# Attention with plain float32 products on quarter and half tiles of the TensorE array, and an instruction order from a list scheduler

## Chip, cores and metric

The kernel runs on one core of a Trainium2 chip. The metric is device time in microseconds (us) of one execution of the whole program; lower is better. Engines are called as in the profile: PE is TensorE's matrix multiply, PEld its weight load, DVE VectorE, ACT ScalarE, POOL GpSimd, SP the queue that issues the transfers.

## What is computed

Sixteen head pairs (4 batches, 8 heads, 576 tokens, 64 features per head) go through attention with a threshold, and the 2304 tokens by 512 features that come out go through two feed-forward layers with 2048 hidden columns. All in float32; weights arrive as float64.

```python
def _attn_ref(q, k, v, tau):
    scale = 1.0 / np.sqrt(q.shape[-1])
    scores = scale * np.matmul(q, k.transpose(0, 1, 3, 2))
    thresh = np.max(scores, axis=-1, keepdims=True) - tau
    scores = np.where(scores >= thresh, scores, -1000000000.0)
    scores = scores - np.max(scores, axis=-1, keepdims=True)
    attn = np.exp(scores)
    attn = attn / (np.sum(attn, axis=-1, keepdims=True) + 1e-09)
    return np.matmul(attn, v).astype(np.float32)

def _moe_ref(x, w_in, w_out):        # first layer
    h = x @ w_in
    g = h * np.cos(h)
    return (g @ w_out).astype(np.float32)

def _moe2_ref(x, w_in, w_out, s, b): # second layer
    h = x @ w_in
    r = np.maximum(h, 0.0)
    g = s * (r * r) + b
    return (g @ w_out).astype(np.float32)
```

## The kernel before

**Attention** (lines 207 to 569). A head pair is one unit of work. Its 1152 queries lie in nine tiles of 128 (tile 4 holds the last 64 queries of both heads). For each tile PE forms the scores against 576 keys in two halves of 288 (`scores`, L368, tile `s`); DVE takes the minimum over the row (`stat`, L380; the scores have their sign turned), a threshold is made from it (`limit`, L389 on DVE or L387 on ACT), ACT takes the exponential (`expo`, L394), and DVE masks it and sums the row in one instruction (`mask`, L406, tile `p`). PE turns `p` through an identity (`transposes`, L460 and L468), ACT copies it out of PSUM (`copies`), and PE multiplies it by the values (`weighted`, L519 for the first head, L528 for the second). The sums go through a reciprocal, a PE transpose and a trip through DRAM (`spread`) to multiply the result (`normalise`, L552 on POOL).

Most products run as float32r passes: an operand x is split into x_hi (rounded) and x_lo = x - x_hi, and the passes are added. For the scores the query's two parts lie on the two halves of the 128 rows (`qs`), the keys lie twice, and two passes per half of the keys do (`kh`, `kl`). For the second head the turned probabilities and the values are split as well (`ph`, `pl`, `vs`). The splits are made on POOL, ACT and DVE (`prep`; `lows`, L509; `pool_high`, `pool_low`). For the first head alone, L519 is a plain float32 product, which fills 64 of the array's 128 columns.

**Layers** (lines 597 to 757). Tokens go in blocks of 512 (one of 256). A step is one block of 128 hidden columns: 12 products into a hidden bank (`hidden`, L662), a chain on DVE, ACT and POOL (`activate`), and 12 products into the accumulators two steps later (`output`, L716 in the first layer, L718 in the second). A layer needs 32 weight halves. Each is loaded as float64 (`wr`), decoded by one ACT and four DVE instructions (`decode`, L157, L159, L161, L165, L169), rounded on ACT (`wh`, L191) and reduced to its low part on POOL (`wl`, L135). Thirteen halves are decoded during attention, 19 of the first layer after it, beside the first block; the second layer's 32 are decoded beside the last block of the first layer and the first block of the second.

**Order.** Every instruction carries a due time from a table of tuned numbers (`ORDER`, `AFTER`, `DEC`, `PACE`), and a heap emits them by that time. Each engine executes its own list strictly in that order. The scores have three PSUM tiles of two banks each, shared with the weighted values; the turned probabilities have two banks.

## Time and profile before

| what | value |
|---|---|
| median of 3 runs | 1205.75 us (1203.57 to 1205.77) |
| span of the profiled execution | 1204.2 us |
| attention, first to last row minimum or mask on DVE | 8.7 to 355 us, 21.6 us per head pair |
| first block of the first layer, to its last output product | 494.7 us |
| from there to the end | 709.5 us |
| busy over the span | PE 94%, DVE 68%, ACT 47%, POOL 46% |

The page gives shares over the whole span, which mixes stages: in attention DVE is busy nearly all of the time and PE nine tenths of it; in the layers PE is busy all of the time, except beside the two stretches in which weights are decoded. So the stages are read apart below. Busy times of PE overlap, since a record's end is modelled: what one product costs is read from the distance between starts.

### The profile page before, as it was taken

To read this page: it belongs to the slowest core of one execution; us is meant where nothing else is said; L and a number is where in the kernel's file an instruction comes from. 1 tells how busy PE (TensorE), PEld (TensorE's weight loads), DVE (VectorE), ACT (ScalarE), POOL (GpSimd) and SP (SyncE) were. 2 spreads that over 40 slices of the span, in tenths; PEclk is the share of its full clock that TensorE was granted. 3 is DMA by queue.
4 is the path that set the end of the run, shared out by engine and by line. 5 is a ranking of instruction groups with operands and counts; after the bars stand their busy time and mean duration, and the time that the engine had idled before them with its cause. 6 is when DMAs were issued, how large, how long until landed. Compare 5 with 4: busy or idle time off the path is not lost.

```text
span 1204.2 us, 16262 instructions
## 1 busy us (share of the span) xinstructions
PE 1129.5 (94%) x5808; PEld 918.3 (76%) x5808; DVE 821.5 (68%) x1410; ACT 568.8 (47%) x1069; POOL 555.3 (46%) x531
## 2 busy tenths in 40 slices
PE   6998888989998888999999999999999999999998
PEld 5676667677675666788998887778888889888886
DVE  7799999999987999645665479998861133212211
ACT  6787777878874444223332244454442233222222
POOL 6687887887865544222222235444542222222221
PEclk9899999999999899999999999999999999999999
DMA  5233333342212232000000012322220000000000
GB/s 155 80 111 110 97 100 121 97 129 92 80 37 80 88 106 90 16 1 1 1 2 1 1 34 94 101 84 91 88 71 1 1 36 1 18 1 1 36 1 35
DMA packets 30416, 68.76 MB, mean 57 GB/s; under 512 B 5232, under 2 KB 9728, under 8 KB 30336
## 3 DMA queue, kind: packets, MB, share of 16 engines
q1 hardware_dynamic: 30192, 67.72, 17.8%
q8 instruction: 46, 0.75, 0.3%
q14 instruction: 34, 0.28, 0.1%
q10 hardware_dynamic: 144, 0.00, 0.0%
HBM read 62.92 MB, written 4.79 MB: 56 GB/s over the span
## 4 chain that ended last, share of the span: by engine, by line
PE 60%; DVE 31%; issue 5%; ACT 2%; DMA 1%; POOL 1%; SPq 0%; DVEq 0%; ACTq 0%; POOLq 0%
PE acc L718 16%; PE hs L662 14%; PE ht L662 13%; PE acc L716 10%; DVE p L406 6%; DVE r L231 5%; DVE mn L380 5%; PE s L368 3%; PE pt L468 3%; DVE wt L161 2%; DVE thr L389 2%; DVE wt L159 2%; DVE wt L169 2%; DVE wt L165 2%; DVE r L679 2%
## 5 line engine op out<-in xcount | busy, mean ns | idle before, releaser
L135 POOL TENSOR_TENSOR gl<-r,gh 128x512 fp32r<-128x512 f32 (+1 forms) x160 | 194.6, 1217 | 435.9 <-DVE gh L231 222.3
L662 PE MATMUL hs<-x,wh 128*128 128x512 f32 (+1 forms) x640 | 187.0, 375 | 20.1 <-DVE r L231 16.2
L679 DVE TENSOR_SCALAR r<-r,s_t,b_t 128x512 f32<-128x512 f32 (+1 forms) x80 | 42.5, 531 | 180.4 <-ACT r L682 180.4
L662 PE MATMUL ht<-x,wh 128*128 128x512 f32 (+1 forms) x560 | 158.6, 368 | 0.0
L662 PEld LDWEIGHTS hs<-x,wh 128*128 128x128 f32 x640 | 117.5, 191 | 47.1 <-DVE r L231 19.0
L368 PE MATMUL s<-kh,qs 128*128 128x288 f32 x320 | 105.7, 346 | 38.1 <-DVE p L406 32.9
L135 POOL TENSOR_TENSOR wl<-wt,wh 128x512 fp32r<-128x512 f32 x60 | 81.4, 1358 | 111.8 <-ACT wh L191 104.8
L662 PE MATMUL hs<-x,wl 128*128 128x512 f32 (+1 forms) x320 | 119.1, 372 | 0.0
L394 ACT ACTIVATE e<-s,mn 128x576 f32<-128x576 f32 x144 | 105.8, 735 | 28.1 <-DVE mn L380 26.7
L716 PE MATMUL acc<-gl,wh 128*128 128x512 f32 (+1 forms) x300 | 111.8, 373 | 6.6 <-POOL gl L135 6.6
L406 DVE SCALAR_TENSOR_TENSOR p<-s,thr,e 128x576 f32<-128x576 f32 x144 | 115.2, 807 | 1.3 <-ACT e L394 0.9
L662 PEld LDWEIGHTS ht<-x,wh 128*128 128x128 f32 x560 | 102.0, 188 | 18.1
L380 DVE TENSOR_REDUCE mn<-s 128x1 f32<-128x576 f32 x144 | 108.2, 752 | 7.8 <-PE s L368 6.3
L682 ACT ACTIVATE r<-r,hpi 128x512 f32<-128x512 f32 (+1 forms) x80 | 54.3, 679 | 122.2 <-DVE r L231 122.2
L716 PE MATMUL acc<-gh,wh 128*128 128x512 f32 (+1 forms) x300 | 111.0, 370 | 0.3 <-ACT gh L682 0.2
L716 PE MATMUL acc<-gh,wl 128*128 128x512 f32 (+1 forms) x300 | 110.6, 369 | 0.0
L368 PEld LDWEIGHTS s<-kh,qs 128*128 128x128 f32 x320 | 63.5, 198 | 59.5 <-issue 26.2
L718 PE MATMUL acc<-wh,gh 128*128 128x512 f32 x270 | 105.2, 390 | 0.0
L718 PE MATMUL acc<-wh,gl 128*128 128x512 f32 x270 | 105.2, 390 | 0.0
L718 PE MATMUL acc<-wl,gh 128*128 128x512 f32 x270 | 105.0, 389 | 0.0
L662 PE MATMUL ht<-x,wl 128*128 128x512 f32 (+1 forms) x280 | 103.0, 368 | 0.0
L468 PE MATMUL pt<-ident,p 128*128 128x128 f32 (+1 forms) x640 | 93.4, 281 | 1.9 <-ACT ph L487 1.2
(97 smaller groups left out, 2399.5 us busy)
## 6 DMA issues: line engine op xcount, KB each, us to landing
wr<-in_w_dram SPq DMA_DIRECT2D x64, 512.0 KB
k<-in_kt_dram SPq DMA_DIRECT2D x32, 288.0 KB
q<-in_qt_dram SPq DMA_DIRECT2D x15, 320.0 KB
q<-in_qt_dram SPq DMA_DIRECT2D x16, 288.0 KB
out_dram<-ob SPq DMA_DIRECT2D x18, 256.0 KB
v<-in_va_dram SPq DMA_DIRECT2D x16, 160.0 KB
v<-in_vb_dram SPq DMA_DIRECT2D x16, 160.0 KB
rb<-rd SPq DMA_DIRECT2D x16, 144.0 KB
```

The costliest lines, as they stand in the source:

```text
L135: (eng or nc.gpsimd).tensor_tensor(out=o, in0=a, in1=b.bitcast(F32), op=ALU.subtract)
L231: heapq.heappush(todo, (key, next(count), lambda: fn(*args)))
L368: nc.tensor.matmul(st[:, h, :H2], qs[:, c : c + 128], kx[:, o + h * H2 : o + (h + 1) * H2], start=(j == 0), stop=(j == len(ops) - 1),)
L380: nc.vector.tensor_reduce(out=mn, in_=sv, axis=mybir.AxisListType.XY, op=ALU.min)
L394: nc.scalar.activation(e, sv, AF.Exp, bias=mn, scale=-1.0)
L406: nc.vector.scalar_tensor_tensor(out=p, in0=sv, scalar=thr, in1=e, op0=ALU.is_le, op1=ALU.mult, accum_out=sm[:, i : i + 1])
L468: nc.tensor.transpose(pt[:kw, j * 128 : (j + 1) * 128], src[:, k * 128 : k * 128 + kw], ident)
L662: nc.tensor.matmul(h, w[:, c * P : (c + 1) * P], x, start=(c == 0 and j == 0), stop=(c == HP - 1 and j == 2))
L679: nc.vector.tensor_scalar(out=o, in0=x, scalar1=a, scalar2=b, op0=ALU.mult, op1=ALU.add)
L682: nc.scalar.activation(o, x, fn, **kw)
L716: nc.tensor.matmul(acc[d][:, :n], w[:, d * P : (d + 1) * P], g, **st)
L718: nc.tensor.matmul(acc[d], g[:, d * P : (d + 1) * P], w, **st)
```

## The change

- All of attention's products become plain float32. No operand of attention is split, so `prep`, `lows`, `pool_high`, `pool_low`, `vc` and `gather` go.
- **Tiles of the array.** The keys' two halves now lie on the two halves of the rows: one product per half contracts 64 rows (tile of 64 rows by 128 columns). Turning is done in pieces of 64 queries, each half of the queries on its half of the rows; the last 64 keys of all tiles are turned by products on quarter tiles (64 by 64, `turn_rest`). The weighted values of the two heads use the two halves of the columns (128 by 64).
- **Places.** The threshold (`limit`), the sums' small addition, the keys' scaling, the weights' clamp and the clamp of the first layer's activation go to POOL. ACT copies all turned probabilities out of PSUM.
- **Buffers.** The scores have two PSUM tiles in place of three, the weighted values one of their own. Eight weight halves have places from the start and are decoded during attention in place of thirteen; the other 24 follow.
- **Order.** A list scheduler (`Order`) places every instruction with a length, a rank, dependences and ring tickets, and emits by planned start.

```diff
+class Order:
...
+    def add(self, engine, length, rank, fn, after=(), take=(), give=(), tail=0):
...
+    def run(self):
...
+EARLY = 8
+PAIR = 14035
...
-    ps_s = ctx.enter_context(tc.tile_pool(name="ps_s", bufs=3, space=PSUM))
+    ps_s = ctx.enter_context(tc.tile_pool(name="ps_s", bufs=2, space=PSUM))
+    ps_v = ctx.enter_context(tc.tile_pool(name="ps_v", bufs=1, space=PSUM))
     ps_t = ctx.enter_context(tc.tile_pool(name="ps_t", bufs=2, space=PSUM))
...
+            def scores(i=i):
+                st = T["s", i] = ps_s.tile([P, 2, 512], F32, tag="s", name=f"s{n}_{i}")
+                parts = [(columns[i], i > mixed)] if i != mixed else [(512, 0), (576, 1)]
+                for j, (c, hd) in enumerate(parts):
+                    for h in range(2):
+                        g = slice(64 * h, 64 * h + 64)
+                        nc.tensor.matmul(
+                            st[:, h, :H2], T["q"][g, c : c + 128], T["ks"][g, hd * H2 : (hd + 1) * H2],
+                            start=(j == 0), stop=(j == len(parts) - 1),
+                        )
...
+            def limit(i=i):
+                T["thr", i] = atiny.tile([P, 1], F32, tag="thr", name=f"thr{n}_{i}")
+                nc.gpsimd.tensor_tensor(out=T["thr", i], in0=T["mn", i], in1=ptau, op=ALU.add)
...
+        def turn(tiles):
...
+            for k in range(4):
+                for j, i in enumerate(tiles):
+                    p = T["p", i].rearrange("p a b -> p (a b)")
+                    for g in range(2):
+                        o = slice(64 * g, 64 * g + 64)
+                        c = (k * len(tiles) + j) * 64
+                        nc.tensor.transpose(pts[g][:, c : c + 64], p[o, k * 128 : k * 128 + 128], ident[o, o])
...
+        def turn_rest():
...
+                        nc.tensor.matmul(
+                            pts[g][64 * hd : 64 * hd + 64, j * 64 : j * 64 + 64], p[o, 512:S], ident[o, o],
+                            start=True, stop=True,
+                        )
...
+        def weighted(h, k):
...
+            for hd in range(2):
+                g = slice(64 * hd, 64 * hd + 64)
+                o = g if k == 4 else slice(0, P)
+                nc.tensor.matmul(
+                    T["av"][g, h, :H2], T["v"][o, hd, k, :],
+                    T["PT"][o, 4 if k == 4 else k + 5 * hd, h * H2 : (h + 1) * H2],
+                    start=(k == 0), stop=(k == 4),
+                )
...
-        nc.vector.tensor_scalar(out=tf, in0=tf, scalar1=TINY, scalar2=None, op0=ALU.max)
+        def clamp():
+            tf = T["t"].bitcast(F32)
+            nc.gpsimd.tensor_scalar(out=tf, in0=tf, scalar1=HUGE, scalar2=TINY, op0=ALU.min, op1=ALU.max)
...
-                (nc.vector.tensor_scalar, r, r, RMAX, RMIN, ALU.min, ALU.max),
+                def s2_():
+                    nc.gpsimd.tensor_scalar(
+                        out=B["r"], in0=B["r"], scalar1=RMAX, scalar2=RMIN, op0=ALU.min, op1=ALU.max
+                    )
...
-    kt = _np.concatenate([kT[:, 0], kT[:, 1]], axis=2)
+    kT = k.reshape(NP, 2, 2, S // 2, D).transpose(0, 2, 4, 1, 3)
...
+    kt = kT.reshape(NP, 128, S)
```

**PE in the middle of attention**, pair 8's fourth to sixth score tile. In the names, `s8_4` is score tile 4 of pair 8, `av7` the weighted values of pair 7, `pt` turned probabilities, `rt` the turned reciprocals. Before:

```order
L460 MATMUL pt7_1_0_2565<-ident_93,p7_4_2281 128x64 x4
L460 MATMUL pt7_1_0_2565<-ident_93,p7_4_2281 64x64
L519 MATMUL av7_0_2571<-ph7_0_2341,v7_0_2369 64x288 x4
L368 MATMUL s8_3_2586<-kh8_2258,qs8_2313 128x288
L368 MATMUL s8_3_2586<-kl8_2426,qs8_2313 128x288
L368 MATMUL s8_3_2586<-kh8_2258,qs8_2313 128x288
L368 MATMUL s8_3_2586<-kl8_2426,qs8_2313 128x288
```

Now:

```order
L315 MATMUL s8_4_2327<-ks8_1935,q8_1933 128x288 x4
L424 MATMUL av7_2334<-PT7_2086,v7_1924 64x288 x2
L393 MATMUL rt7_2337<-ident_104,r7_2257 9x128
L315 MATMUL s8_5_2341<-ks8_1935,q8_1933 128x288 x2
L424 MATMUL av7_2334<-PT7_2086,v7_1924 64x288 x2
L278 MATMUL pt8_0_0_2361<-ident_104,p8_0_2253 128x64
L278 MATMUL pt8_0_1_2362<-ident_104,p8_0_2253 128x64
```

A score tile takes two products where it took four passes; products of the two heads' weighted values alternate and are spread between score tiles; a turn has pieces of 64 columns.

**DVE at the same place.** `mn` is the row minimum, `p` the masked tile, `wt` a weight half. Before:

```order
L380 TENSOR_REDUCE mn8_6_2611<-s8_6_2606 128x1
L406 SCALAR_TENSOR_TENSOR p8_3_2625,sm8_2530<-s8_3_2586,thr8_3_2593,e8_3_2614 128x576
L509 TENSOR_TENSOR pl7_2474<-pt7_1_0_2565,ph7_1_2473 128x4x64
L509 TENSOR_TENSOR ph7_1_2473<-pt7_1_0_2565,ph7_1_2473 64x64
L509 TENSOR_TENSOR ph7_1_2473<-pt7_1_5_2594,ph7_1_2473 64x512
L380 TENSOR_REDUCE mn8_5_2663<-s8_5_2627 128x1
L406 SCALAR_TENSOR_TENSOR p8_6_2666,sm8_2530<-s8_6_2606,thr8_6_2613,e8_6_2634 128x576
L389 TENSOR_TENSOR thr8_5_2665<-mn8_5_2663,ptau_66 128x1
L159 TENSOR_SCALAR wt0_2_1_2599<-wt0_2_1_2599 128x512
```

Now:

```order
L322 TENSOR_REDUCE mn8_4_2339<-s8_4_2327 128x1
L322 TENSOR_REDUCE mn8_5_2354<-s8_5_2341 128x1
L544 SCALAR_TENSOR_TENSOR wt0_2_0_2265<-wr0_2_0_1314,wt0_2_0_2265 128x512
L336 SCALAR_TENSOR_TENSOR p8_4_2388,sm8_2252<-s8_4_2327,thr8_4_2356,e8_4_2358 128x576
L336 SCALAR_TENSOR_TENSOR p8_5_2402,sm8_2252<-s8_5_2341,thr8_5_2382,e8_5_2384 128x576
L322 TENSOR_REDUCE mn8_6_2425<-s8_6_2404 128x1
L322 TENSOR_REDUCE mn8_7_2435<-s8_7_2427 128x1
```

Minima and masks stand two by two, one for each of the two score tiles, with a weight instruction between in every second pair; subtractions and thresholds are gone.

**DVE in the first block of the first layer.** `r0_0_6` is step 6's activation, `hs`, `ht0` and `h1` hidden banks. Before:

```order
L231 TENSOR_TENSOR r0_0_5_5315<-hs_4789,r0_0_5_5315 128x512
L679 TENSOR_SCALAR r0_0_6_5374<-ht0_5002 128x512
L231 SCALAR_TENSOR_TENSOR r0_0_6_5374<-r0_0_6_5374,ht0_5002 128x512
L231 TENSOR_SCALAR r0_0_6_5374<-r0_0_6_5374 128x512
L169 SCALAR_TENSOR_TENSOR wt0_9_1_5336<-wr0_9_1_5290,wt0_9_1_5336 128x512
L159 TENSOR_SCALAR wt0_11_0_5385<-wt0_11_0_5385 128x512
L161 TENSOR_SCALAR wt0_11_0_5385<-wt0_11_0_5385 128x512
L165 SCALAR_TENSOR_TENSOR wt0_11_0_5385<-wr0_11_0_5334,wt0_11_0_5385 128x512
```

Now:

```order
L685 TENSOR_TENSOR r0_0_5_4790<-h0_4422,r0_0_5_4790 128x512
L664 TENSOR_SCALAR r0_0_6_4846<-h1_4423 128x512
L534 TENSOR_SCALAR wt0_6_1_4821<-wt0_6_1_4821 128x512
L539 SCALAR_TENSOR_TENSOR wt0_6_1_4821<-wr0_6_1_4795,wt0_6_1_4821 128x512
L544 SCALAR_TENSOR_TENSOR wt0_6_1_4821<-wr0_6_1_4795,wt0_6_1_4821 128x512
L674 SCALAR_TENSOR_TENSOR r0_0_6_4846<-r0_0_6_4846,h1_4423 128x512
```

One instruction of four is gone from each step (the clamp of `r`) and one of four from each half (the clamp of `wt`). At step 6 the halves being decoded are those of column block 6, where they were those of block 9 to 11.

## Rows read from the trace of the kernel before

**Rows 1.** Page, part 1: busy us (share of the span) xinstructions
```profile
PE 1129.5 (94%) x5808; PEld 918.3 (76%) x5808; DVE 821.5 (68%) x1410; ACT 568.8 (47%) x1069; POOL 555.3 (46%) x531
```
**Rows 2.** Windows: stretch, us; busy PE, PEld, DVE, ACT, POOL (x), PEclk, DMA, GB/s
```profile
60.00:340.00 280.00, 252.69 (x1645) 195.41 (x1644) 277.63 (x534) 222.48 (x462) 225.48 (x244) 1.00 0.33 103
371.50:492.00 120.50, 97.94 (x386) 75.00 (x386) 113.51 (x147) 51.52 (x83) 59.09 (x43) 0.94 0.28 91
...
713.00:892.00 179.00, 172.40 (x753) 140.17 (x752) 163.46 (x229) 82.93 (x137) 84.28 (x62) 1.00 0.28 89
```
**Rows 3.** Timeline of DVE inside attention: start us, us, what
```profile
208.32 0.76 DVE L380 TENSOR_REDUCE mn<-s 128x1 f32<-128x576 f32 x1
208.99 0.81 DVE L406 SCALAR_TENSOR_TENSOR p<-s,thr,e 128x576 f32<-128x576 f32 x1
...
209.73 0.75 DVE L380 TENSOR_REDUCE mn<-s 128x1 f32<-128x576 f32 x1
```
**Rows 4.** Timeline of PE: plain float32 on 64 columns, then float32r scores
```profile
211.58 2.15 PE L519 MATMUL av<-ph,v 128*64 128x288 f32 x8
213.66 0.40 PE L368 MATMUL s<-kh,qs 128*128 128x288 f32 x1
213.90 0.29 PE L368 MATMUL s<-kl,qs 128*128 128x288 f32 x1
```
**Rows 5.** Timeline of PE: passes that fill 128 columns, and turns of 64 columns
```profile
200.80 0.43 PE L528 MATMUL av<-pl,vs 128*128 128x288 f32 x2
201.07 0.42 PE L528 MATMUL av<-ph,vs 128*128 128x288 f32 x2
...
201.60 0.60 PE L468 MATMUL pt<-ident,p 128*64 128x128 f32 x4
202.13 0.51 PE L460 MATMUL pt<-ident,p 64*128 64x64 f32 x5
202.57 0.53 PE L528 MATMUL av<-ph,vs 128*128 128x288 f32 x2
```
**Rows 6.** DVE's groups in 371.5 to 492 us: busy us, mean ns
```profile
L165 DVE SCALAR_TENSOR_TENSOR wt<-wr,wt 128x512 int32<-128x512 int32 x19 | 21.0, 1105 | 0.5
L231 DVE TENSOR_SCALAR r<-r 128x512 f32<-128x512 f32 x17 | 17.3, 1018 | 0.3
L159 DVE TENSOR_SCALAR wt<-wt 128x512 f32<-128x512 f32 x19 | 17.2, 907 | 0.5 <-ACT wt L157 0.5
L169 DVE SCALAR_TENSOR_TENSOR wt<-wr,wt 128x512 int32<-128x512 int32 x19 | 16.0, 840 | 0.4
L161 DVE TENSOR_SCALAR wt<-wt 128x512 int32<-128x512 int32 x19 | 10.3, 540 | 0.5
```
**Rows 7.** Line 161 over the whole run: ns min/median/max
```profile
L161 DVE TENSOR_SCALAR wt<-wt x64: 411/428/1530, 66.3 to 889.5; 128x512 int32<-128x512 int32 x64
```
**Rows 8.** POOL's groups over the run, moved clamp's nearest row and low part
```profile
L132 POOL TENSOR_SCALAR ph<-pf 128x512 fp32r<-128x512 f32 x48 | 30.7, 640 | 52.4 <-ACT pf L476 44.9 <-DVE xs L548 7.3
L135 POOL TENSOR_TENSOR wl<-wt,wh 128x512 fp32r<-128x512 f32 x60 | 81.4, 1358 | 111.8 <-ACT wh L191 104.8 <-DVE r L231 4.1 <-PE acc L716 2.9
```
**Rows 9.** Timeline at the start: keys scaled, first score passes, first minimum
```profile
4.39 0.77 ACT L273 ACTIVATE kh<-k,f_t 128x576 fp32r<-128x576 f32 x1 [1.72 <-DVE qs L135]
...
6.47 0.44 PE L368 MATMUL s<-kh,qs 128*128 128x288 f32 x1
...
6.71 0.44 PE L368 MATMUL s<-kl,qs 128*128 128x288 f32 x1
...
8.70 0.74 DVE L380 TENSOR_REDUCE mn<-s 128x1 f32<-128x576 f32 x1
```
**Rows 10.** Timeline at attention's end: last mask on DVE, last normalise on POOL
```profile
354.17 0.82 DVE L406 SCALAR_TENSOR_TENSOR p<-s,thr,e 128x576 f32<-128x576 f32 x1
...
371.63 1.44 POOL L552 TENSOR_TENSOR xT<-xs,rb 128x576 f32<-128x576 f32 x1 [5.34 <-PE hs L662]
```
**Rows 11.** Window of line 716 alone: the first block's 192 output products
```profile
360.00:494.70 134.70, 50.98 (x192) 37.03 (x192) 0.95 0.27 85
```

1064 lines of the change are left out of this document (501 added, 563 removed), and 19 rows, old and new, of the table ORDER.

## Prediction

> **What bounds the kernel now.** I read the page's first part, then the stages. Over the span PE is busy 94% and DVE 68% [rows 1], which mixes stages. The windows part them [rows 2]. From 60 to 340 us DVE works 277.6 of 280 us (99%), PE 252.7 (90%), ACT and POOL some 80%: attention is bound by DVE. Beside the first block (371.5 to 492 us) DVE works 113.5 of 120.5 us and PE 97.9: again DVE, now with weight halves. From 713 to 892 us PE loses 6.6 of 179 us. Elsewhere in the layers PE is the bound, and the change leaves its products alone.
>
> The first minimum starts at 8.7 us [rows 9] and the last mask ends at 355.0 [rows 10]: 346.3 us for 16 pairs, 21.6 us each. The first block's 192 output products are done at 494.7 us [rows 11]; from there to the end of the span, 1204.2 us, are 709.5 us. The question is what a pair costs after, and what follows the last mask. I count in P, the period of a pair.
>
> **DVE per pair, after.** Minima and masks stay. In the timeline a minimum takes its place for 0.67 us (208.32 to 208.99) and a mask with its sum 0.74 (208.99 to 209.73) [rows 3]; nine of both are 12.7 us, with a reciprocal of 0.2 some 12.9. Subtractions, thresholds and gather leave. Ten halves are now decoded on DVE by the last mask, three instructions each. Beside the first block the three cost 1.105 + 0.840 + 0.540 = 2.49 us [rows 6]; line 161, the shortest, has a median of 0.43 and goes up to 1.53 [rows 7], so three times 0.43 is the low end. Ten halves are 13 to 25 us, 0.8 to 1.6 a pair. DVE's floor is 13.7 to 14.5 us, I take 14.1, not 21.6.
>
> **PE per pair, after.** Prices by distance of starts: eight plain float32 records take 2.08 us (211.58 to 213.66), 0.26 each, and a product is two records, 0.52 us [rows 4]; a float32r pass is 0.13 (two in 0.27, 200.80 to 201.07); four turns of 128 columns take 0.53, 0.13 each (201.60 to 202.13), five of 64 columns 0.44, 0.088 each (to 202.57) [rows 5]. After a change of the array's shape the first step is longer: 0.24 instead of 0.13 at 213.66 [rows 4], so 0.11 us a change. These prices give the pair of before: 40 score passes 5.2, 20 plain records 5.2, 18 passes 2.4, 40 turns of 128 columns 5.2 and ten of 64 0.9, some twelve changes 1.3: 20.2 us; the window shows 252.7 / 280 of 21.6, which is 19.5. So they hold within 4%.
>
> After, by the order: 20 score products, 74 turns of 64 columns, 16 quarter-tile products (32 records, priced as the turns, 0.088), 20 weighted products, and some 14 changes of shape. One after another: 10.4 + 6.5 + 2.8 + 0.1 + 10.4 + 1.6 = 31.8 us. If tiles that share no rows or no columns run at the same time: 5.2 + 3.3 + 0.7 + 0.1 + 5.2 + 1.6 = 16.1 us. No row of before has two such tiles side by side, so these are the two ends. Nearest are the passes that fill all 128 columns: 0.13 us [rows 5], a quarter of a plain product's 0.52 on 64 columns [rows 4], so twice the width costs a pass no time. The array does work on both halves in one stream; that two instructions can do so is what the rows lack. I take the lower end, with 0.5 us a pair for in-order waits: P = 16.6. The Trainium skill (TensorEngine Tiling (Array Packing), Key Properties) says that different tiles may load weights and multiply in parallel; no row here shows it. By that rule P would be the lower end, without it the upper.
>
> ACT has no split left and as many copies; its 222.5 of 280 us [rows 2] are 17.2 us a pair, of which some 4 go (keys, thresholds, the second head's copies). POOL keeps the keys' scaling, normalise and small sums, and loses all splits. Neither is the bound, though each can hold a mask: POOL's threshold stands behind normalise in its list, and a mask waits for it.
>
> **Start and attention.** The keys' scaling starts at 4.39 and takes 0.77 us; at the start a pass takes 0.24 us (6.47 to 6.71) [rows 9], so three records of twice that, 1.44, and signals bring the first minimum to some 6.9 us, where it was 8.7 because a second split came first. The last mask ends at 6.9 + 16 x 16.6 = 272.5 us.
>
> **From the last mask to the layers.** Before, normalise of the last pair ends at 373.1 us, 18.1 after the last mask [rows 10]. After, the same kinds of steps stand there: the last turns, the last pair's weighted products, three hidden groups of the first block between them, copy-out, normalise. Weighted products cost PE less, no split waits between, but more hidden groups come first: I keep 18.0. Only then are the activation's places free; the hidden groups count as done.
>
> **The first block.** DVE's busy time there was 113.5 us for 19 halves, 17 activations and four token splits. Out go the clamp of r, 17.3, and that of wt, 17.2 [rows 6]; the groups add up to 5% more than the busy time, so they are worth 32.8: 80.7 us. Twenty-two halves remain after the ten, three more than before, at 2.49 us: 7.1 with the same 5%. That is 87.8 us. Against it, POOL gains a clamp for every half and step, 0.64 us each [rows 8], and goes from 59 of 120 us to some 81 of 95. DVE's SBUF instructions are long when POOL works: line 161 costs 0.43 or up to 1.53 [rows 7], and line 165 a mean of 1.1 in this stretch [rows 6]. Ends: 88 us if that doesn't grow, and 124 if each of 66 decode instructions waits half a low part, 0.55 us, longer. I take 98, nearer to the lower end since an instruction right behind another doesn't wait anew. PE worked 97.9 us in that stretch [rows 2] and has less left in it, as hidden groups are done by then, so DVE still decides. With 2.7 us for the last half's way to the products (492 to 494.7): 100.7.
>
> **The rest** is 709.5 us. The second layer's decode loses a DVE clamp per half as well; of the 6.6 us that PE waits there I take 3: 706.5.
>
> Sum: 272.5 + 18.0 + 100.7 + 706.5 = 1097.7 us of span. The profiled execution lies 1.5 us under the median of 1205.75, so I forecast 1099 us; in general 6.9 + 16 P + 825.2 + 1.5. Known to be uncertain by -10 to +26 us for the first block at the same P.
>
> **Rivals.**
>
> *DVE is the bound.* Changes of shape and waits hide behind the other tile, PE falls under DVE's 14.1 us. For it: PE's sum is only 2.0 us above, and a change costs 0.11 us by a single kind of step. Against: two score buffers only, so a score product stands in the way between mask and next minimum. P = 14.1: 1059 us.
>
> *Records keep their order.* In the timeline PE's records start in program order without exception. A product's two records must follow each other on their tile, so the second tile's first record starts no sooner than the first tile's second: a lone pair takes three records, 0.78 us, not 0.52. At some 14 groups a pair that is 14 x 0.26 = 3.6 us: P = 20.2, 1157 us. The Trainium skill (TensorE: Matmul & The Clock Gate, What overlaps and what doesn't) has matmuls start and end strictly in program order and only weight loads pulled ahead. By that rule the time would be this rival's, unless the following turns fill the gap. Against: turns do follow most score tiles, and runs of four to eight weighted products fill themselves.
>
> *Tiles don't overlap for plain float32, so the change doesn't do what it is laid out for.* PE needs 31.8 us a pair where float32r needed 19.5. P = 31.8: 1342 us, slower. It decides from P = (1204.2 - 825.2 - 6.9) / 16 = 23.3 us, that is when less than 56% of the 15.2 us come that the overlap is worth; in part, as with one of the two kinds of tiles, it ends between 1200 and 1270. For it: nothing in the trace shows two tiles at once, and a plain record (0.26) is two float32r passes. Against: only the full-width passes above.
>
> *POOL holds the masks.* Normalise waits for the trip through DRAM, and thresholds queue behind it. At 2 us a pair it adds 32: 1131. It lies within the forecast's range.
>
> **How the numbers follow.** Forecast, with POOL's case (P 15 to 18.5, 1072 to 1135): 0.45. DVE's bound: 0.20. Records in order: 0.17. No or half an overlap: 0.17, of which a tenth ends under the time of before, and 0.01 ends at it. Faster by over 0.2%: 0.82; within 0.2%, about what a measurement of this kernel can tell from no change: 0.01; slower: 0.17. The range holds 8 in 10 from 1048 (DVE's bound, with the first block at its lower end) to 1190 (records in order, with the first block at its upper end and some waits); it leaves out the case without overlap and a little at both ends.
>
> **What would show it.** Right: in the profile after, the two products of a score tile start 0.26 us apart or less and end within 0.8 us; pairs repeat every 16 to 17 us; PE is over 90% busy and DVE some 85% in attention; the first block's last output product comes some 118 us after the last mask, with DVE above 90% there. Wrong: PE rows one after another at 0.26 us each (no overlap); DVE at 99% in attention (its bound); PE waiting at score products for a mask that waited for POOL. The sum fails if the change of shape costs much more than 0.11 us, or if ACT's strided copies take much longer than its contiguous ones.

## The result and the profile after

The changed kernel takes 1216.14 us (median of 4, 1213.36 to 1216.64) where the kernel before takes 1204.68 in the same session (1203.57 to 1205.77): ratio 1.0089, 95% interval 1.0075 to 1.0103. It is slower by 0.9%; 1099 us was forecast, and the range (1048 to 1190) doesn't hold the time. The profiled execution has a span of 1213.9 us.

The page's first part of the changed kernel, busy us (share of the span) xinstructions, which answers to [rows 1]:

```profile
PE 1106.7 (91%) x6736; PEld 831.3 (68%) x6736; DVE 648.1 (53%) x1102; ACT 499.0 (41%) x903; POOL 452.6 (37%) x573
```

DVE lost 173 us of work, POOL 103, ACT 70: the work did leave, and the program became longer all the same. By stages (the table below), the end of attention comes 28 us earlier than before, and what follows it takes 38 us longer: 2.5 to the last normalise, 3.6 in the first block, 26.7 in the rest of the first layer and 4.8 in the second. The windows of the changed kernel, by stage (columns as in [rows 2]):

```profile
60.00:320.00 260.00, 225.71 (x2453) 125.26 (x2451) 190.89 (x388) 171.97 (x336) 69.87 (x176) 0.95 0.27 85
347.60:472.40 124.80, 102.69 (x375) 77.44 (x374) 95.83 (x122) 53.16 (x84) 85.16 (x83) 0.89 0.30 93
472.40:690.00 217.60, 213.87 (x1109) 181.67 (x1108) 93.54 (x161) 62.67 (x114) 79.68 (x95) 1.00 0.02 6
690.00:816.40 126.40, 110.05 (x443) 86.51 (x442) 103.13 (x124) 54.79 (x89) 86.19 (x80) 0.95 0.29 92
```

In attention (first line) DVE went from 99% to 73%, PE from 90% to 87%: now **no engine is full**. The same holds beside the first block (second line: PE 82%, DVE 77%, POOL 68%) and beside the second stretch of decode (fourth line). Only the third stretch has a bound, PE.

The table splits every run's profiled execution at the same events: P is the time from the start of the first row minimum to the end of the last mask, over 16; then to the end of the last normalise; to the end of the first block's 192nd output product; to the end of the first layer's last one; and to the end of the span. (The expectations count the first block 0.5 us shorter, to the end of its 190th product: 124.8 us there is 125.2 here.) All in us; times without an interval are single executions.

| kernel | P | to normalise | first block | first layer's rest | second layer | time |
|---|---|---|---|---|---|---|
| before | 21.64 | 18.1 | 121.6 | 317.3 | 392.4 | 1204.68 |
| prediction | 16.6 | 18.0 | 100.7 | 706.5 together | | 1099 |
| after | 20.02 | 20.6 | 125.2 | 343.9 | 397.1 | 1216.14 |
| x1 products of a score tile on the same rows | 29.32 | | | | | 1363.3 |
| x2 12 of 20 weighted products left out | 17.95 | 18.2 | 126.9 | 342.6 | 396.9 | 1180.4 |
| x3 threshold on DVE | 21.31 | 19.2 | 125.3 | 342.3 | 396.9 | 1233.2 |
| x4 both clamps on DVE | 20.56 | 20.2 | 125.8 | 373.1 | 393.0 | 1249.8 |
| x5 mask off the score tiles | 17.41 | 20.1 | 124.8 | 345.9 | 399.1 | 1177.4 |
| x6 clamp of r on DVE | 20.02 | 20.8 | 132.4 | 352.8 | 399.7 | 1234.4 |
| x7 planner's lengths as measured | 19.20 | 19.3 | 124.7 | 343.9 | 397.0 | 1200.8 |
| x8 three score tiles, one lent | 21.86 | 22.9 | 124.9 | 344.5 | 396.7 | 1247.3 |
| x9 second decode later | 20.01 | 20.6 | 125.0 | 326.4 | 400.5 | 1201.2 |
| x10 three raw places | 19.88 | 20.1 | 124.4 | 354.2 | 392.7 | 1218.1 |
| x11 = x5 + x7 + x9 | 16.72 | 20.0 | 124.0 | 328.0 | 402.5 | 1150.9 |
| x12 as x11, ranks chosen anew | 16.54 | 18.1 | 131.4 | 320.5 | 396.5 | 1139.0 |
| x13 = x9 with three raw and decoded places | 20.32 | 20.5 | 117.9 | 330.6 | 405.1 | 1207.7 |
| x14 = x9 with weights' low part on DVE | 20.36 | 20.0 | 123.5 | 322.2 | 396.9 | 1196.9 |
| x15 as after, ranks chosen anew | 18.93 | 17.7 | 128.8 | 320.6 | 400.7 | 1179.8 |

Against the forecast, attention is 55 us long (16 x 3.42), the way to normalise 2.6, the first block 24.5, the rest 34.5: 116 us of span, with 0.2 us of gain at the start.

**One turn through attention** shows what replaced the bound. This is the timeline of the changed kernel (start us, us, instruction, idle time before and its releaser):

```profile
142.75 0.75 POOL L260 TENSOR_SCALAR ks<-k,f_t 128x576 f32<-128x576 f32 x1 [2.27 <-PE s L315]
...
143.46 1.41 POOL L446 TENSOR_TENSOR xT<-xs,rb 128x576 f32<-128x576 f32 x1
...
144.82 0.34 POOL L326 TENSOR_TENSOR thr<-mn,ptau 128x1 f32<-128x1 f32 x2
145.05 0.82 DVE L336 SCALAR_TENSOR_TENSOR p<-s,thr,e 128x576 f32<-128x576 f32 x1 [0.95 <-POOL thr L326]
...
146.02 0.76 PE L315 MATMUL s<-ks,q 64*128 64x288 f32 x4 [2.11 <-DVE p L336]
...
147.08 0.74 PE L315 MATMUL s<-ks,q 64*128 64x288 f32 x4
...
147.85 0.76 DVE L322 TENSOR_REDUCE mn<-s 128x1 f32<-128x576 f32 x1 [0.16 <-PE s L315]
...
148.91 0.75 ACT L330 ACTIVATE e<-s,mn 128x576 f32<-128x576 f32 x1
...
149.69 0.76 PE L315 MATMUL s<-ks,q 64*128 64x288 f32 x4
...
149.76 0.82 DVE L336 SCALAR_TENSOR_TENSOR p<-s,thr,e 128x576 f32<-128x576 f32 x1 [0.29 <-ACT e L330]
...
150.64 1.24 PE L315 MATMUL s<-ks,q 64*128 64x288 f32 x8
```

Two things are to be seen. First the round through a score tile: products at 147.08, minimum at 147.85, exponential at 148.91, mask at 149.76, and only when the mask has read the scores do the next products go into that tile, at 150.64: 3.56 us (the other tile: 146.02 to 149.69, 3.67). With two tiles, nine score tiles a pair need 9 x 3.6 / 2 = 16.2 us even if nothing else stands in the way. That is as long as PE's own work of 16.1 us by the prediction's sum. Second, in the first rows, POOL: the thresholds stand behind the keys' scaling and normalise, DVE's mask waits 0.95 us and PE 2.11.

Since PE executes in order, what it does in the round's gaps can also be too long for them. From the same kernel's timeline:

```profile
135.22 2.46 PE L424 MATMUL av<-PT,v 128*64 128x288 f32 x16
...
137.60 0.76 PE L315 MATMUL s<-ks,q 64*128 64x288 f32 x4
...
138.41 0.76 DVE L322 TENSOR_REDUCE mn<-s 128x1 f32<-128x576 f32 x1 [1.52 <-PE s L315]
```

Both score tiles were free from 136.9 us at the latest, but eight weighted products stood ahead of the next score. The waits of 60 to 320 us (us in total, times, longest) add this up:

```profile
DVE mn L322 <- PE s L315: 54.2, 90, 2.6
ACT e L330 <- DVE mn L322: 40.7, 53, 2.6
...
PE s L315 <- DVE p L336: 16.9, 14, 2.2
...
DVE p L336 <- POOL thr L326: 5.7, 6, 0.9
```

DVE waits for PE and PE for DVE: a closed round of three engines, not an engine. Waits of masks for POOL's thresholds, the last line, are small: 5.7 us, 0.4 a pair.

What a pair's 20.02 us hold follows from the first window above, 260 us or 13.0 pairs: PE is busy for 17.4 us a pair and idle for 2.6. The granted clock has a mean of 0.95 there, where it was 1.00 before [rows 2]. A tenth of the time at half the clock makes at most 1.0 of the 17.4 us (an estimate), so PE's work at the full clock is 16.3 us or a little more, near the 16.1 of the sum. The experiments below are split in the same way.

### The profile page after: what moved, and what is told of

Read it like the earlier page. It is cut to its first block, busy times and chain, and to the rows that moved or that the text cites. A ratio compares the mean times of both kernels' runs of the same rounds, so it can differ in the third digit from the quotient of the medians.

```text
span 1213.9 us, 17640 instructions
## 1 busy us (share of the span) xinstructions
PE 1106.7 (91%) x6736; PEld 831.3 (68%) x6736; DVE 648.1 (53%) x1102; ACT 499.0 (41%) x903; POOL 452.6 (37%) x573
## 3 DMA queue, kind: packets, MB, share of 16 engines
q1 hardware_dynamic: 23280, 63.00, 16.1%
## 4 chain that ended last, share of the span: by engine, by line
PE 66%; DVE 15%; POOL 7%; issue 6%; ACT 5%; DMA 1%; SPq 0%; DVEq 0%; POOLq 0%; ACTq 0%
PE h L641 26%; PE acc L736 15%; PE acc L734 9%; PE s L315 7%; PE av L424 6%; DVE wt L539 3%; DVE wt L544 3%; PE pt L278 2%; DVE wt L534 2%; POOL wl L186 2%; ACT e L330 2%; POOL gl L186 2%; DVE mn L322 1%; DVE p L336 1%; DVE r L664 1%
## 5 line engine op out<-in xcount | busy, mean ns | idle before, releaser
L641 PE MATMUL h<-x,wh 128*128 128x512 f32 (+1 forms) x1280 | 380.5, 383 | 28.6 <-DVE r L685 10.9
L641 PEld LDWEIGHTS h<-x,wh 128*128 128x128 f32 x1280 | 238.0, 193 | 82.2 <-ACT wh L557 10.4
L641 PE MATMUL h<-x,wl 128*128 128x512 f32 (+1 forms) x640 | 244.8, 383 | 2.1 <-POOL wl L186 2.0
L315 PE MATMUL s<-ks,q 64*128 64x288 f32 x640 | 125.4, 482 | 41.9 <-DVE p L336 29.1
L641 PEld LDWEIGHTS h<-x,wl 128*128 128x128 f32 x640 | 123.8, 193 | 28.2 <-POOL wl L186 4.1
L223 ACT ACTIVATE r<-h 128x512 f32<-128x512 f32 (+1 forms) x80 | 44.5, 556 | 239.4 <-PE h L641 217.4
L734 PE MATMUL acc<-gh,wh 128*128 128x512 f32 (+1 forms) x320 | 120.9, 378 | 4.1 <-ACT gh L223 2.7
L315 PEld LDWEIGHTS s<-ks,q 64*128 64x128 f32 x640 | 57.3, 203 | 78.5 <-issue 52.4
L685 DVE TENSOR_TENSOR r<-h,r 128x512 f32<-128x512 f32 (+1 forms) x80 | 50.6, 634 | 109.4 <-PE h L641 70.9
L424 PE MATMUL av<-PT,v 128*64 128x288 f32 (+1 forms) x640 | 101.8, 426 | 0.0
```

What stands on the lines that cost most here:

```text
L223: nc.scalar.activation(o, x, fn, **kw)
L315: nc.tensor.matmul(st[:, h, :H2], T["q"][g, c : c + 128], T["ks"][g, hd * H2 : (hd + 1) * H2], start=(j == 0), stop=(j == len(parts) - 1),)
L424: nc.tensor.matmul(T["av"][g, h, :H2], T["v"][o, hd, k, :], T["PT"][o, 4 if k == 4 else k + 5 * hd, h * H2 : (h + 1) * H2], start=(k == 0) ...
L641: nc.tensor.matmul(h, w[:, c * P : (c + 1) * P], x, start=(c == 0 and j == 0), stop=(c == HP - 1 and j == 2))
L685: nc.vector.tensor_tensor(B["r"], B["h"], B["r"], ALU.mult)
L734: nc.tensor.matmul(acc[d][:, :n], w[:, d * P : (d + 1) * P], g, **st)
```

## The experiments

The theory after the first comparison: the tiles of the array work as priced; attention is held by the round through two score tiles together with the order of PE's queue. Its rivals: PE's records keep their order, so PE itself has 20 us of work (the prediction's rival, whose 20.2 us happens to be the measured P); POOL's thresholds and the low clock that follows them; a bad order alone. For the layers: DVE's load against the order.

**x1: are tiles side by side at all?** Every score product on the lower rows.

```diff
-                        g = slice(64 * h, 64 * h + 64)
+                        g = slice(0, 64)
```

> Both products of a score tile are put on the lower 64 rows of the array instead of one on each half; the order stays as it was, and the scores are not the reference's (the second half of the keys is left out, the first used twice). If the two row tiles really work at the same time (a pair of products 0.56 to 0.60 us from start to start in the changed kernel's timeline) and TensorE's time is on the path: a pair of products goes to four records of 0.26, 1.04 us, ten of them a head pair, +4.6 us a pair, 74 us in all: 1290 us (1260 to 1295). If row tiles bring nothing, or TensorE's time is not on the path: 1216 us.

1363.3 us. Timeline where the granted clock is 1.00 and where it is 0.50, and the window of 60 to 460 us:

```profile
115.64 1.23 PE L315 MATMUL s<-ks,q 64*128 64x288 f32 x4
```
```profile
107.24 4.21 PE L315 MATMUL s<-ks,q 64*128 64x288 f32 x8
```
```profile
60.00:460.00 400.00, 369.14 (x2608) 213.61 (x2605) 204.35 (x412) 183.78 (x358) 75.00 (x187) 0.77 0.19 61
```

Four records take 1.23 us here, 0.76 on two row tiles: 0.47 us a tile, about the 4.6 us a pair of the expectation. So the overlap is real. The other 4.7 us of the 9.3 were not expected: the granted clock has a mean of 0.77, and eight records at 107.24 us take 4.21 us, nearly twice the time. PE was busy 92% of that stretch.

**x2: does PE's time count?** Weighted products of three of five key blocks left out.

```diff
-            for hd in range(2):
+            for hd in range(2 if k in (0, 4) else 0):
```

> Of the 20 weighted products a head pair the 12 of the second, third and fourth block of keys are left out (the result is not the reference's); everything else, the order too, stays. TensorE gets 12 x 0.29 = 3.5 us a pair less to do. If TensorE's own time sets the pair (records keep their order, 20 us of work): P falls from 20.0 to 16.5, 56 us less: 1160 us. If the chain from score to minimum, exponential, mask and back through two score tiles sets it: under 1 us a pair, 1200 to 1216 us.

P is 17.95: of 3.5 us taken from PE 2.1 came. Neither theory alone: PE's work counts in part, and with less of it PE waits more. It is busy 77% of the time (176.09 of 230 us from 60 us on), so its idle time grew from 2.6 to 4.2 us a pair.

**x3: threshold on DVE.**

```diff
-                nc.gpsimd.tensor_tensor(out=T["thr", i], in0=T["mn", i], in1=ptau, op=ALU.add)
+                nc.vector.tensor_tensor(out=T["thr", i], in0=T["mn", i], in1=ptau, op=ALU.add)
```

> The threshold of each score tile is made on VectorE instead of GpSimd; the planner is told so. If thresholds queued behind normalise and the keys' scaling are what stops TensorE every second pair (2.1 us without work, then some 7 us at half the clock, eight times: 8 x (2 + 3) = 40 us): 1175 us, and no stretch of attention at the granted clock 0.5. If masks wait for thresholds only in the place of another wait, since no engine is full: 1205 to 1220 us, with clock dips as before.

1233.2 us, worse than either. The line's group in 60 to 340 us (ns min/median/max), and the window:

```profile
L326 DVE TENSOR_TENSOR thr<-mn,ptau x119: 158/159/1401, 63.0 to 338.9; 128x1 f32<-128x1 f32 x119
```
```profile
60.00:340.00 280.00, 232.72 (x2481) 131.64 (x2479) 217.74 (x509) 170.80 (x339) 48.91 (x60) 0.91 0.26 81
```

Nine thresholds of 0.16 us are 1.4 us a pair, 2.0 by their mean of 0.22, since some take 1.4 us beside POOL's normalise. P rose by 1.3, though DVE has 22% of its time free: PE's idle time by 1.0 us a pair and its busy time by 0.3, at a granted clock of 0.91. So work added to an engine of the round lengthened the pair; how much is the threshold's length and how much the clock isn't parted. POOL's stalls at thresholds are gone and P is not shorter, but DVE's work came in their place, and the low clock stayed. So this run alone doesn't clear them. The 5.7 us of waits above say that they cost 0.4 us a pair directly; what a stall costs beyond that, by the lower clock after it, lies within the 1.0 us a pair worked out above. (The expectation counted eight stretches of some 7 us at half the clock; a mean of 0.95 over 260 us holds four.)

**x5: take the mask out of the round.** The mask compares exp(min - s) with exp(-tau) instead of the score with its threshold.

```diff
-                    out=p, in0=T["s", i][:, :, :H2], scalar=T["thr", i], in1=T["e", i], op0=ALU.is_le, op1=ALU.mult,
+                    out=p, in0=T["e", i], scalar=etau, in1=T["e", i], op0=ALU.is_ge, op1=ALU.mult,
...
-            t_ = add("POOL", 150, at + PLACE["stat"], limit, after=[m_], take=[th])
-            e_ = add("ACT", 735, at + PLACE["exp"], expo, after=[m_], take=[te], give=[tm])
+            e_ = add("ACT", 735, at + PLACE["exp"], expo, after=[m_], take=[te], give=[tm, ts])
```

> The mask compares the exponential with exp(-tau) instead of the score with minimum plus tau, so it no longer reads the scores: a score's PSUM tile comes free after the exponential, not after the mask, and the 144 thresholds on GpSimd go. The order is planned anew with that. If the round through two score tiles sets the pair (3.56 us from one score product to the next in the same tile at 147.08 to 150.64 us, of which the mask is 0.9): the round falls to some 2.6 us, P to 17 to 18 us and the time to 1168 to 1185 us. If TensorE's own sequence sets it (records in order, 20 us of work): P stays within 0.5 us of 20, 1205 to 1217 us.

1177.4 us, P 17.41, as the round's theory had it.

```profile
60.00:280.00 220.00, 206.14 (x2377) 110.89 (x2375) 184.93 (x372) 163.07 (x323) 48.49 (x54) 1.00 0.30 95
```

Of the 2.6 us a pair that were gained 1.5 are PE's idle time (2.6 to 1.1) and 1.1 its busy time (17.4 to 16.3), with the granted clock at 1.00 again. A part of PE's sequence that needs 20 us of its own is excluded. Threshold and mask left together here, so their shares aren't measured apart; the waits of masks for POOL's thresholds were 0.4 us a pair.

**x7: the planner's lengths.** Scores 560 ns and 130 until readable (520), weighted 590 (490), turns 310 a tile (280), mask 820 (890).

```diff
-                "PE", 490, end + PLACE["weigh"] + j * PLACE["weigh_step"], lambda h=h, k=k: weighted(h, k),
+                "PE", 590, end + PLACE["weigh"] + j * PLACE["weigh_step"], lambda h=h, k=k: weighted(h, k),
```

> Only the lengths in the planner are set to what the trace shows: a score product pair 0.56 us plus 0.13 until its result can be read (planned 0.52), a pair of weighted products 0.59 (0.49), turns 0.31 a tile (0.28), a mask 0.82 (0.89). If wrong lengths made the order bad: P falls by 0.5 to 1.5 us, 1192 to 1208 us. If the order is not what costs: 1210 to 1222 us.

P 19.20, 1200.8 us: the same instructions in a better order gain 0.8 us a pair, about half of it waits; the granted clock is 0.97.

**x8: three score tiles, one lent to the weighted values.**

```diff
-    ps_s = ctx.enter_context(tc.tile_pool(name="ps_s", bufs=2, space=PSUM))
-    ps_v = ctx.enter_context(tc.tile_pool(name="ps_v", bufs=1, space=PSUM))
+    ps_s = ctx.enter_context(tc.tile_pool(name="ps_s", bufs=3, space=PSUM))
...
-        ts = ticket("av")
+        ts = ticket("s")
```

> The scores get three PSUM tiles, one of which the weighted values use in turn, as in the kernel before; the order is planned anew. If the round through two tiles alone sets the pair: three tiles, of which one is lent to the weighted values for about a third of the pair, make it 1.3 times as wide: P 17 to 18.5 us, 1165 to 1190 us. If the lent tile stops the scores for as long as it is lent (weighted products, 5.9 us, and their copy), P is 20 to 22 us: 1215 to 1250 us.

1247.3 us, P 21.86. PE's timeline shows why:

```profile
121.69 0.71 PE L423 MATMUL av<-PT,v 128*64 128x288 f32 x4
122.33 0.71 PE L277 MATMUL pt<-ident,p 64*128 64x64 f32 x16
122.97 2.46 PE L423 MATMUL av<-PT,v 128*64 128x288 f32 x16
125.36 0.71 PE L277 MATMUL pt<-ident,p 64*128 64x64 f32 x16
126.00 1.68 PE L423 MATMUL av<-PT,v 128*64 128x288 f32 x12
...
128.69 1.67 PE L314 MATMUL s<-ks,q 64*128 64x288 f32 x10
```

The planner put 18 of a pair's 20 weighted products and over half of its turns into one run of 7 us without a score; DVE's next minimum waits 5.17 us. The run says nothing on how wide three tiles would be in a good order: it stays open.

**x15: the order alone**, with the changed kernel's instructions, the lengths as in x7 and x12, and new ranks.

```diff
-    "scores": -4612, "stat": 383, "exp": -3692, "mask": 1952, "turn": 2851, "turned": 3471, "rest": 398,
...
-    "keys": -7358, "early": 3.855, "early_step": 2.038, "first": -1.881, "second": -1.98, "decode": 0,
+    "scores": -17538, "stat": -5856, "exp": -7908, "mask": 6049, "turn": -3370, "turned": 18533,
...
+    "normalise": 28462, "keys": -7946, "early": 3.964, "early_step": 2.274, "first": -0.361, "second": 10.854,
```

> The changed kernel's instructions, nothing else than planner's lengths and ranks chosen anew, for these instructions, in the way of x12; the mask reads the scores again. If the order is what costs: P falls towards x12's 16.54, 17.5 us or less, 1135 to 1160 us. If the round of score, minimum, exponential and mask through two tiles holds a pair in any order: P stays at 19 us or more (x7 had 19.20), and only the layers gain: 1165 to 1190 us.

P 18.93, just under the 19 that was expected; 1179.8 us (ratio to before 0.9808, 0.9781 to 0.9834). With the mask in the round none of the three orders that ran (after, x7, x15) comes under 18.9. So of the 3.4 us a pair that were missing a new order brings 1.1, and taking mask and threshold out as well, with ranks chosen anew, 2.4 more (x12: 16.54). The windows of both runs, shown with x12, say what kind of time that is. PE's busy and idle us a pair are 17.4 and 2.6 in the changed kernel, 16.5 and 2.4 in x15, 16.2 and 0.4 in x12: the order gave back the full clock (0.95 to 0.99) and little waiting, and the waits went with the mask. PE's waits at scores, x15 from 60 to 300 us and x12 from 60 to 260:

```profile
PE s L315 <- DVE p L336: 16.9, 18, 2.4
```
```profile
PE s L317 <- ACT e L328: 3.9, 12, 0.4
```

In x15 they add up to 16.9 us, as in the changed kernel; PE's other waits there, 12 us, stand mostly at turns, for ACT's copies. That no order with the mask in the round does better isn't shown.

**x4 and x6: the clamps.** x4 has both clamps on DVE, x6 that of r alone.

```diff
-            nc.gpsimd.tensor_scalar(out=tf, in0=tf, scalar1=HUGE, scalar2=TINY, op0=ALU.min, op1=ALU.max)
+            nc.vector.tensor_scalar(out=tf, in0=tf, scalar1=HUGE, scalar2=TINY, op0=ALU.min, op1=ALU.max)
...
-                    nc.gpsimd.tensor_scalar(
+                    nc.vector.tensor_scalar(
                         out=B["r"], in0=B["r"], scalar1=RMAX, scalar2=RMIN, op0=ALU.min, op1=ALU.max
```

> The weights' clamp and the clamp of the activation go from GpSimd back to VectorE, as in the kernel before; the rest stays. If the two stretches with decode are bound by the chain that crosses one more engine (ScalarE, GpSimd, VectorE): the 125 us from the last normalise to the first block's end fall by 15 to 25 us and the second stretch by 10: 1175 to 1195 us. If VectorE's load decides there, as the prediction had it, the clamps cost 33 us in the first and 15 in the second stretch: 1250 to 1265 us.

> Only the clamp of the first layer's activation goes back from GpSimd to VectorE; the weights' clamp stays on GpSimd. It tells which of the two edits of x4 cost its 33.6 us. If VectorE's load in the stretches with decode is what counts: half of it, 1225 to 1238 us. If the weights' clamp, which stands in the decode of 64 halves, made it: 1200 to 1215 us, since ScalarE waits for GpSimd's clamp of r 24 us in 440 to 500 us alone and that wait goes.

1249.8 and 1234.4 us. In the first block neither theory of x4 held: with both clamps on DVE it takes 125.8 us, neither 15 to 25 less nor 33 more. The window of that stretch in x4:

```profile
356.10:481.40 125.30, 98.56 (x374) 68.35 (x373) 117.84 (x160) 52.70 (x85) 55.94 (x42) 0.99 0.31 93
```

DVE is 94% busy there, against 77% in the changed kernel, for the same 125 us: 22 us of work came to DVE, and as much of its waiting went. With the clamp of r alone (x6) the block takes 132.4. Of x4's loss 29 us lie in the second stretch of decode (373.1 against 343.9) and 9 in attention (P 20.56), whose cause is open. In the second stretch DVE's queue holds the activations up (between 680 and 860 us PE's products wait 33.2 us for DVE's `r`, and the weight loads, largely at the same time, 36.6).

**x9: the second stretch's order.** One rank.

```diff
-    "keys": -7358, "early": 3.855, "early_step": 2.038, "first": -1.881, "second": -1.98, "decode": 0,
+    "keys": -7358, "early": 3.855, "early_step": 2.038, "first": -1.881, "second": 10, "decode": 0,
```

> One number of the planner is changed: the second layer's weight halves get a rank 12 steps later (second: 10 in place of -1.98), so on VectorE, ScalarE and GpSimd the activations of the first layer's last blocks come before a half's decode where both are ready. If the 26.7 us that blocks 2 to 5 of the first layer take longer than before come from decode instructions standing ahead of activations: the stretch from the first block's end to the end of the first layer falls from 343.9 to 320 to 330 us, 1190 to 1202 us in all, nothing changes ahead of it. If GpSimd's or VectorE's load makes it: no change, 1210 to 1220 us.

1201.2 us; 326.4 in place of 343.9, and nothing changes ahead of it; the second layer takes 3.4 us more. The timeline of the changed kernel shows what the rank did (DVE, ACT and POOL first, then PE):

```profile
740.30 0.69 DVE L539 SCALAR_TENSOR_TENSOR wt<-wr,wt 128x512 int32<-128x512 int32 x1
...
741.03 1.66 DVE L544 SCALAR_TENSOR_TENSOR wt<-wr,wt 128x512 int32<-128x512 int32 x1
...
742.62 1.28 DVE L685 TENSOR_TENSOR r<-h,r 128x512 f32<-128x512 f32 x2
...
743.39 0.63 ACT L223 ACTIVATE gh<-r 128x512 fp32r<-128x512 f32 x1
...
743.43 1.28 POOL L186 TENSOR_TENSOR wl<-wt,wh 128x512 fp32r<-128x512 f32 x1 [1.29 <-ACT wh L557]
...
744.67 1.27 POOL L186 TENSOR_TENSOR gl<-r,gh 128x512 fp32r<-128x512 f32 x1
```
```profile
744.07 0.50 PE L734 MATMUL acc<-gh,wh 128*128 128x512 f32 x1 [0.83 <-ACT gh L223]
745.99 0.50 PE L734 MATMUL acc<-gl,wh 128*128 128x512 f32 x1 [1.42 <-POOL gl L186]
```

The later of two sines ended on ACT at 739.94 us; both activations `r` were ready for DVE then, and stood behind two decode instructions till 742.62; then `gl` stood behind `wl` on POOL. PE waited for both. The half that went first is not needed until a block later.

**x10, x13, x14: the first block.** Three places for the raw halves (x10), for the decoded ones too (x13, whose line is shown first), and the low part on DVE (x14). x13 and x14 hold x9's rank as well. In all three a block's output groups are chained in order, and x10 and x13 make room by writing low parts of the tokens over each other.

```diff
-        ("rb", 2), ("xs", 2), ("wr", 2), ("wt", 2), ("r", 2), ("gh", 2), ("gl", 2), ("mn", 6), ("thr", 6),
+        ("rb", 2), ("xs", 2), ("wr", 3), ("wt", 3), ("r", 2), ("gh", 2), ("gl", 2), ("mn", 6), ("thr", 6),
```
```diff
-            psub(W[half][1], T["t"].bitcast(F32), W[half][0])
+            psub(W[half][1], T["t"].bitcast(F32), W[half][0], nc.vector)
```

> Three places for the raw float64 halves instead of two; to make room the low part of the tokens' fourth quarter is written over the third's (a small loss of precision), and the output groups of a block are chained in order. If the first block is bound by the round of a raw place (transfer, absolute value, clamp, three VectorE instructions, then the next transfer: two halves in flight): the stretch from the last normalise to the first block's end falls from 124.8 to 108 to 116 us. If VectorE's or GpSimd's load binds it: 122 us or more. In all 1195 to 1207 us against 1212 to 1220.

> As x9 (second: 10), with three places for the raw halves and three for the decoded ones; to make room the low parts of the tokens' last three quarters share one place (a small loss of precision), and a block's output groups are chained in order. If the first block is bound by the round through two places, now that of the decoded half, which is held from the absolute value to the end of GpSimd's low part: the stretch from the last normalise to the first block's end falls from 124.5 to 105 to 115 us. If an engine's work with its mutual slowing binds it: 120 us or more.

> As x9 (second: 10), with the weights' low part made on VectorE (0.7 us estimated from the 0.68 us of its subtraction at the tokens) in place of GpSimd (1.29 to 1.62); output groups chained. If GpSimd binds the first block, by its 1.3 us in each half's chain and by the slow VectorE instructions beside it (1.0 to 1.7 us where 0.43 to 0.69 is the least): the first block's stretch falls from 124.5 to 100 to 115 us, and lines of the shift, sign and fill go to 0.45 to 0.75 us. If VectorE's load binds it: 24 x 0.7 = 17 us more, 135 to 142 us.

124.4, 117.9 and 123.5 us against 125. Three raw places alone do nothing. Three of both bring 7 us, under the 10 to 20 of the round's theory, and the program as a whole is no faster than x9 (1207.7 against 1201.2). With POOL's low part gone, DVE has 104.87 us of work instead of 95.83 and the block takes no more time. No single place, engine or chain was found that holds this block. The groups of DVE in it, changed kernel (busy us, mean ns, idle before and releaser):

```profile
L544 DVE SCALAR_TENSOR_TENSOR wt<-wr,wt 128x512 int32<-128x512 int32 x22 | 24.0, 1089 | 0.7
...
L539 DVE SCALAR_TENSOR_TENSOR wt<-wr,wt 128x512 int32<-128x512 int32 x22 | 22.5, 1021 | 0.7
...
L534 DVE TENSOR_SCALAR wt<-wt 128x512 int32<-128x512 int32 x22 | 15.2, 692 | 14.6 <-POOL wt L531 14.6
...
L685 DVE TENSOR_TENSOR r<-h,r 128x512 f32<-128x512 f32 x18 | 12.3, 683 | 15.0 <-ACT r L223 12.8 <-PE h L641 2.3
```

Most of DVE's 29 us without work stand behind the two clamps that were moved off it: 14.6 us for `wt` directly, 12.8 for the sine behind the clamp of `r`. But x4, where both clamps are back, is no shorter, so these waits aren't shown to be what holds the block.

**x11 and x12: the edits together.** x11 is x5, x7 and x9 in one. x12 has the decode's lengths from the trace as well and ranks chosen anew.

```diff
-    "scores": -4612, "stat": 383, "exp": -3692, "mask": 1952, "turn": 2851, "turned": 3471, "rest": 398,
...
+    "scores": -13300, "stat": 11128, "exp": 20031, "mask": 21475, "turn": 7358, "turned": -13960,
```

> The edits of x5 (mask off the scores), x7 (lengths) and x9 (second layer's decode later) together. If they act in separate places, they add up: P 17.2 us or less, 320 to 330 us from the first block's end to the end of the first layer, and 1140 to 1160 us. If the lengths bring nothing once the round through the score tiles is short: P as in x5, 17.4, and 1152 to 1165 us.

> As x11, with the decode's lengths in the planner also set to the trace (GpSimd's low part 1.38 us, VectorE's three 0.6, 1.1, 1.2) and the planner's ranks chosen anew for these lengths. TensorE's own 16.1 to 16.6 us a pair should then be the bound of attention: P 16.5 to 17.2, the first block 112 to 122 us, the first layer's rest 317 to 328 us: 1120 to 1145 us. If ranks matter little: as x11, 1140 to 1160 us.

1150.9 us, then 1139.0 us (1138.64 to 1139.95; ratio to before 0.9458, 0.9442 to 0.9474): faster than both kernels. The windows of 60 to 260 us in x12 and of 60 to 300 us in x15:

```profile
60.00:260.00 200.00, 195.76 (x2299) 107.54 (x2292) 180.41 (x363) 156.80 (x316) 50.20 (x55) 1.00 0.34 104
```
```profile
60.00:300.00 240.00, 209.05 (x2410) 117.12 (x2405) 187.75 (x380) 167.71 (x331) 68.35 (x172) 0.99 0.28 92
```

In x12 PE is the bound at last, 98% busy at the full clock, with P at 16.54 us. Its first block takes 131.4 us, outside the 112 to 122 expected and 10 us longer than before; DVE has 110 us of work there instead of 96, as sign and fill (lines 539 and 544 of the changed kernel) take 1.34 and 1.22 us in the mean instead of 1.02 and 1.09. Why the new order slows them is open. The exact ranks carry no lesson; that a new choice of ranks came to a P of 16.54 us without the mask in the round, and to 18.93 with it (x15), does.

## Why the prediction was wrong, step by step

- **Start: right.** First minimum at 6.7 us (6.9).
- **PE's price list and the overlap: right.** A lone pair of score products takes 0.76 us to the minimum, pairs in a run follow each other by 0.56 to 0.60, x1 shows 0.47 us a tile as the price of giving the row overlap up, and x12 runs at the 16.1 us of the sum plus 0.4. As the prediction asked, a score tile's two products start together: of the four records from 146.02 us on, two have started by 146.10 (window of tile `s` alone), where in x1, with both products on the same rows, the four from 115.64 us on start one by one:

```profile
146.00:146.10 0.10, 0.08 (x2) 1.00 1.27 233
```

  The Trainium skill (TensorEngine Tiling (Array Packing), Key Properties) has different tiles multiply in parallel; these rows agree, for two row tiles in plain float32.
- **"With 0.5 us a pair for in-order waits: P = 16.6": this step failed**, by 3.4 us a pair or 55 us, the largest miss. The 0.5 us stood for everything that isn't an engine's work; measured, PE was idle for 2.6 us a pair, and its own work was 17.4 in place of 16.1, up to 1.0 of it from a fall of the clock that the sum didn't have. The round through two score tiles was never added up, although its terms could be had before the change: 0.76 for the minimum and 0.81 for the mask [rows 3], a product pair, and the exponential from the page of before:

```profile
L394 ACT ACTIVATE e<-s,mn 128x576 f32<-128x576 f32 x144 | 105.8, 735 | 28.1 <-DVE mn L380 26.7
```

  With the hand-offs that is 3.6 us as measured after, times 9, over two tiles, 16.2 us. Two limits of 16 us that share an in-order queue didn't give 16: x15 and x12, with and without the mask in the round, differ by 2.4 us a pair (18.93 and 16.54). The sum used busy time per engine only, and "two score buffers only" was named as a remark against DVE's rival, without a price.
- **The rival "records keep their order" gave 20.2 us and P is 20.02**; the agreement is an accident. A lone pair does last 0.76 where the rival had 0.78, but its products start together and not a record apart, and x5 and x12 run the same records at 17.41 and 16.54. The Trainium skill (TensorE: Matmul & The Clock Gate, What overlaps and what doesn't) has matmuls start and end in program order; no row here speaks against it, and that order alone did not make the time.
- **"POOL holds the masks", 2 us a pair: seen in the timeline, at a fifth of the price.** Masks wait for thresholds 5.7 us in 60 to 320 us, 0.4 a pair, not counting what the clock loses after a stall.
- **Last mask to normalise: nearly right**, 20.6 against 18.0.
- **The first block: DVE's work was right, "so DVE still decides" was wrong.** DVE has 95.8 us of work there; 98 was taken for the stretch. It lasted 125.2. The clamps lie in both chains, of the half and of the activation, and DVE's waits stand behind them; but x4 takes them back and gains nothing, so what holds the block stays open. PE, said to have less than [rows 2]'s 97.9 us left, had 102.7, at a granted clock of 0.89.
- **The rest: wrong by 34.5 us**, where 3 us of gain had been counted for a clamp less on DVE. The new order puts second-layer halves ahead of activations (x9 takes 17.5 us of it back with one number, x12 23.4). The order had been read in attention and in the first block, and not here. The second layer's 4.8 us over before have no experiment.
- **Slips of arithmetic that change nothing above:** by the prediction's own formula P 15 to 18.5 gives 1074 to 1130 us, where 1072 to 1135 stands, and its cases give chances of 0.84 for faster and 0.14 for slower, where 0.82 and 0.17 stand.

So the instructions do what they were priced at. What failed is that they were taken to run as a full queue, with the list scheduler's order as given. Attention gained 26 us of the 81 forecast, and what follows it lost 38, so the program came out slower.

## What to carry to other kernels

When a change takes work off the fullest engine, add up the closed rounds too: for each ring of buffers the time from one filling to the next through all engines, divided by the number of places, against each engine's sum; where two come out alike, expect neither to be reached. What counts there is an instruction's place in the round, not only whether its engine has time: moving the threshold to another engine of the round (x3) made the pair longer, taking mask and threshold out of it (x5) made it 2.6 us shorter. And feed a planner the lengths that the trace shows: its order is only as good as they are, here 0.8 us of 20 a pair, and one wrong priority 15 us of the whole.

## What the runs showed of the hardware

- **The granted clock fell after PE had stood still, but not every time.** Windows of the changed kernel around two gaps of 2.1 us:

```profile
103.00:105.40 2.40, 0.29 (x11) 0.18 (x7) 1.45 (x4) 2.19 (x4) 1.60 (x4) 1.00 0.87 256
105.40:106.60 1.20, 1.20 (x22) 1.11 (x24) 1.00 (x3) 0.00 (x0) 0.14 (x1) 1.00 0.77 303
106.60:113.40 6.80, 6.25 (x53) 3.23 (x52) 3.54 (x8) 4.12 (x8) 0.57 (x3) 0.51 0.04 14
...
143.90:146.00 2.10, 0.01 (x1) 0.01 (x1) 1.15 (x4) 1.92 (x4) 1.29 (x4) 1.00 0.85 230
146.00:153.00 7.00, 6.04 (x79) 3.63 (x81) 5.64 (x12) 4.24 (x9) 0.92 (x5) 1.00 0.18 62
```

  After the first gap PE runs 6.8 us at 0.51, the 1.2 GHz level; after the second it stays at 2.4. In attention the mean is 0.95, so a tenth of 260 us, 26 us, ran at the lower level, which cost at most 13. In x1, with both products on the lower rows, PE was 92% busy and the mean was 0.77. What decides stays open.
- **DVE instructions with two inputs in SBUF took longer beside POOL.** In the changed kernel's first block the fill (line 544) takes 0.69 us at least and 1.67 at most; one starts at 403.13 us and takes 1.64, while POOL's low part runs from 402.79 to 404.23. In x12 a mask with both inputs in SBUF takes 1.44 us beside normalise, 0.81 else. The Trainium skill (SBUF — State Buffer, Who interferes with whom) says that such an instruction contends with a GpSimd instruction that reads SBUF; the rows agree. Moving POOL's low part away (x14) took the means of sign and fill in the first block from 1.02 and 1.09 us to 0.86 and 0.85; the shift (line 534) went from 0.69 to 0.88, so not every line gained.
